# Weight conversion spread over VectorE, ScalarE and GpSimd, and two elementwise steps moved to GpSimd, in an mLSTM cell with a multiplicative feed-forward block

## The chip, the cores and the metric

The kernel runs on one core of a Trainium2 chip. The core has five engines that run their own instruction streams in order: TensorE (PE, with its weight loads shown as PEld), VectorE (DVE), ScalarE (ACT), GpSimd (POOL) and SyncE (SP), which issues all DMA transfers of this kernel. The metric is device time of one execution in microseconds; lower is better. A profile is one execution recorded by the hardware profiler; its time is given beside its span.

## The reference

Two blocks follow each other. The first is an mLSTM cell over 4 batches, 8 heads, 768 steps and head dimension 40:

```python
for t in range(S):
    m_new = np.maximum(f_gate[:, :, t] + m, i_gate[:, :, t])
    f_stab = np.exp(f_gate[:, :, t] + m - m_new)
    i_stab = np.exp(i_gate[:, :, t] - m_new)
    C = f_stab * C + i_stab * np.einsum('bhd,bhe->bhde', vt, kt)
    n = f_stab * n + i_stab * kt
    h_tilde = np.einsum('bhde,bhe->bhd', C, qt)
    denom = np.maximum(np.abs(np.einsum('bhd,bhd->bh', n, qt)), 1.0)
    y[:, :, t] = sigmoid(o_gate[:, :, t]) * h_tilde / denom
```

Its output, as 3072 tokens of 320 features, goes through `((x @ w1) * (x @ w2)) @ w3 @ w_out` with a hidden width of 1024. The activations come as float32. The four weight matrices come as float64 and are turned into float32 on the chip.

## The kernel before, in words

**Units.** The sequence is cut into 6 chunks of 128 steps (two halves of 64) for each of 4 batches: 24 units, unit n being chunk n // 4 of batch n % 4. For a unit, `load` fetches k, q and v, and `load_u` fetches into `pw` a broadcast row of stabilised gate sums. `weights` turns `pw` into decay weights: eight Exps on ScalarE (L221) and two masks on GpSimd (L223). `turn` transposes k and q on TensorE. `scores` multiplies them into PSUM (`ss`) and multiplies by `pw` on VectorE (L243). `cell` scales v by gate weights on GpSimd (`vw`, L257), forms the chunk's contribution to the state (`pc`), decays the state on GpSimd (L268) and adds on VectorE (L271), applies q to the state (`pi`) and the scores to v (`ph`), and adds the two in `h` (L284, L291). Then it forms the denominator's reciprocal (L295 to L298), multiplies the sigmoid of the output gate by it (L300), and multiplies `h` by that product into `y` (L302). GpSimd copies the tail of `y` (L304), and `x_trans` transposes `y` into `xT`.

**Gates.** `gates_of` runs scans over the forget and input gates on VectorE, first for the first 128 steps, then for the other 640. It ends in three differences and sums (L367, L368, L372), whose transposes on TensorE give `aT` and `wT`, the biases and weights that the units use.

**Weights.** `fetch` loads a piece of float64 weights as pairs of 32-bit words into one of three `raw` buffers. `convert` calls `to_f32`, which takes the exponent (`ex`) and the mantissa (`ma`, with the low word added) apart by bit operations and multiplies them into the float32 destination: seven passes on VectorE (L146 to L152). There are 34 such pieces: ten of w1 and w2, 512 columns wide, eight of w_out, 320 wide, and sixteen of w3, 512 wide. A w3 piece is transposed (`w3_trans`) and multiplied with w_out (`w3_mm`), so that the block's last two products become one with `w3o`.

**Feed-forward.** `ffn_up` computes one 128-wide slice of the hidden layer for a group of four units (`pa`, `pb`; copy on ScalarE, L428; product on VectorE, L429). `ffn_out` multiplies by `w3o` and stores.

**Order.** A loop over 30 steps writes units, conversions (list `n_cvt`), `ffn_up` and `ffn_out` (lists `n_up`, `n_down`) side by side; a planner in the tile framework then orders each engine's stream by its own estimate of durations and adds the semaphores. Streams are in order, so an instruction waits for all that stands ahead of it on its engine. Three things tie the steps together: `ss`, `pc` and `pi` share one PSUM buffer; qT, kT, vw and y have two buffers each; and a load waits in SyncE's queue until its buffer is free, with all later loads behind it.

Of the kernel before, what the change touches and what calls it, by code (L numbers as in the profile page):

```python
# [8 lines left out]
FP = mybir.dt.float32  # L9
U32 = mybir.dt.uint32  # L10
AF = mybir.ActivationFunctionType
OP = mybir.AluOpType
# [3 lines left out]
def kernel(  # L16
# [25 lines left out]
    nc = tc.nc  # L42

    B, H, S, D = q.shape
    L = 64
    P = 128
# [7 lines left out]
    BH = B * H  # L54
# [8 lines left out]
    const = ctx.enter_context(tc.tile_pool(name="const", bufs=1))  # L63
# [62 lines left out]
    wr = const.tile([2 * REM, DFF], FP, name="wr")  # L126
    w3o = const.tile([128, FO, DM], FP, name="w3o")
    CW = 512
    w1_d, w2_d, w3_d, wo_d = (x.bitcast(U32) for x in (moe_w1, moe_w2, moe_w3, moe_w_out))

    def raw_tile(n, pieces):
# [5 lines left out]
    def to_f32(dst, raw):  # L137


        n = dst.shape[-1]  # L140
        lo, hi = raw[:, :, 0], raw[:, :, 1]
        ex = wst.tile([128, n], U32, name="ex", tag="ex", bufs=1)
        ma = wst.tile([128, n], U32, name="ma", tag="ma", bufs=1)
        mf = ma.bitcast(FP)
        V = nc.vector
        V.tensor_scalar(out=ex, in0=hi, scalar1=20, scalar2=0x7FF, op0=OP.logical_shift_right, op1=OP.bitwise_and)  # L146
        V.tensor_scalar(out=ex, in0=ex, scalar1=896.0, scalar2=0.0, op0=OP.subtract, op1=OP.max)
        V.tensor_scalar(out=ex, in0=ex, scalar1=254.0, scalar2=float(1 << 23), op0=OP.min, op1=OP.mult)
        V.scalar_tensor_tensor(out=ex, in0=hi, scalar=0x80000000, in1=ex, op0=OP.bitwise_and, op1=OP.bitwise_or)  # L149
        V.tensor_scalar(out=ma, in0=hi, scalar1=0xFFFFF, scalar2=0x100000, op0=OP.bitwise_and, op1=OP.bitwise_or)  # L150
        V.scalar_tensor_tensor(out=mf, in0=lo, scalar=2.0 ** -32, in1=ma, op0=OP.mult, op1=OP.add)  # L151
        V.scalar_tensor_tensor(out=dst, in0=mf, scalar=2.0 ** -20, in1=ex.bitcast(FP), op0=OP.mult, op1=OP.mult)  # L152

    def cols(c0, n):
        return slice(2 * c0, 2 * (c0 + n))
# [89 lines left out]
    def cell(n):  # L245
        c, b = divmod(n, B)
        pw, vt, kt = u_t.pop(n), vbuf[n % NB], kbuf[n % NB]
        qT = qT_t.pop(n)
        first, second, after = state[b]
        state[b] = after, second, first  # L250
        hs = slice(b * H, (b + 1) * H)
        quarters = ((0, 0), (1, 1), (0, 1), (1, 0))


        ends = range(2 if c < NT2 - 1 else 1)
        vw = sb.tile([P, H, D1], FP, name="vw", tag="vw")
        nc.gpsimd.tensor_tensor(out=vw, in0=vt, in1=wT[:, c, hs].unsqueeze(2).to_broadcast([P, H, D1]), op=OP.mult)  # L257
        _, pc = two_banks("pc", D1)
        for p in range(NP):
            for x, e in quarters:  # L260
                if x in ends:
                    nc.tensor.matmul(pc[halves[e], x, p, :], lhsT=kt[halves[x], 2 * p + e, :],  # L262
                                     rhs=vw[halves[x], 2 * p + e, :], start=True, stop=True)

        def next_state(new, old, x):
            c1 = 2 * c + x - (2 if c else 0)
            if (c, x) > (0, 0):
                nc.gpsimd.tensor_tensor(out=new, in0=old, op=OP.mult,  # L268
                                        in1=dec_of[min(c, 1)][:, b * NP:(b + 1) * NP, c1:c1 + 1]
                                        .to_broadcast([P, NP, D1]))  # L270
                nc.vector.tensor_tensor(out=new, in0=pc[:, x], in1=new, op=OP.add)  # L271
            else:
                nc.vector.tensor_copy(out=new, in_=pc[:, x])

        next_state(second, first, 0)
        if len(ends) > 1:
            next_state(after, second, 1)
        h = sb.tile([P, H, D1], FP, name="h", tag="h")
        _, pi = two_banks("pi", D1)
        for p in range(NP):  # L280
            for hip, x in quarters:
                r, t = halves[hip], halves[x]
                nc.tensor.matmul(pi[t, hip, p, :], lhsT=qT[r, p, t], rhs=(first, second)[x][r, p, :], start=True, stop=True)  # L283
        nc.vector.tensor_tensor(out=h.rearrange("p (n two) d -> p two n d", two=2), in0=pi,  # L284
                                in1=gT[:, c, hs].rearrange("p (n two) -> p two n", two=2).unsqueeze(3)
                                .to_broadcast([P, 2, NP, D1]), op=OP.mult)
        ph = tps([P, H, D1], "ph")
        for hd in range(H):
            for r in halves:
                nc.tensor.matmul(ph[r, hd, :], lhsT=pw[r, hd, :], rhs=vt[r, hd, :], start=True, stop=True)  # L290
        nc.vector.tensor_tensor(out=h, in0=ph, in1=h, op=OP.add)  # L291


        den = sb.tile([P, H, 1], FP, name="den", tag="den")
        nc.vector.tensor_scalar(out=den.bitcast(U32), in0=h[:, :, D:D1].bitcast(U32), scalar1=0x7FFFFFFF, scalar2=None,  # L295
                                op0=OP.bitwise_and)
        nc.vector.tensor_scalar(out=den, in0=den, scalar1=1.0, scalar2=None, op0=OP.max)
        nc.vector.reciprocal(out=den, in_=den)  # L298
        e = o_t[n // GT][:, n % GT]
        nc.vector.tensor_tensor(out=e, in0=e, in1=den.to_broadcast([P, H, D]), op=OP.mult)  # L300
        y_t[n] = sb.tile([P, DM + REM], FP, name="y", tag="y")
        nc.vector.tensor_tensor(out=y_t[n][:, 0:DM].rearrange("p (h d) -> p h d", d=D), in0=h[:, :, 0:D], in1=e,  # L302
                                op=OP.mult)
        nc.gpsimd.tensor_copy(out=y_t[n][:, DM:DM + REM], in_=y_t[n][:, KF * P:DM])  # L304
# [12 lines left out]
    with tc.tile_pool(name="gates", bufs=1) as gates:  # L317
        f_sb = gates.tile([BH, S], FP, name="f_sb")
        a = gates.tile([BH, S], FP, name="a")
# [30 lines left out]
        def gates_of(c0, c1, then=None):  # L350
            n = c1 - c0
            rs = slice(c0 * L, c1 * L)
            f3, F3, U3, a3, w3d = (x.rearrange("p (c t) -> p c t", t=L)[:, c0:c1] for x in (f_sb, F, U, a, w))
            nc.vector.tensor_tensor_scan(out=F[:, rs], data0=on[:, rs], data1=f_sb[:, rs], initial=0.0,
                                         op0=OP.mult, op1=OP.add)

            nc.vector.memset(f3[:, :, 0:1], -1.0e30)
            nc.vector.tensor_tensor_scan(out=U[:, rs], data0=f_sb[:, rs], data1=a[:, rs], initial=0.0,
                                         op0=OP.add, op1=OP.max)
            nc.vector.tensor_tensor_scan(out=M[:, c0 + 1:c1 + 1], data0=F3[:, :, L - 1], data1=U3[:, :, L - 1],  # L360
                                         initial=M[:, c0:c0 + 1], op0=OP.add, op1=OP.max)
            before = M[:, c0:c1].unsqueeze(2).to_broadcast([BH, n, L])
            nc.vector.tensor_tensor(out=U3, in0=U3, in1=before, op=OP.subtract)
            nc.vector.tensor_tensor(out=U[:, rs], in0=U[:, rs], in1=F[:, rs], op=OP.max)
            last = nc.vector.tensor_tensor(out=U[:, rs], in0=F[:, rs], in1=U[:, rs], op=OP.subtract)
            nc.sync.dma_start(out=(U_rest if c0 else U_first).rearrange("c r t -> r c t"), in_=U3)
            nc.vector.tensor_tensor(out=a3, in0=a3, in1=before, op=OP.subtract)  # L367
            nc.vector.tensor_tensor(out=a[:, rs], in0=a[:, rs], in1=F[:, rs], op=OP.subtract)  # L368
            gate_cols(a, aT, c0 // 2, c1 // 2)
            if then:  # L370
                then()
            nc.vector.tensor_tensor(out=w3d, in0=a3, in1=U3[:, :, L - 1:L].to_broadcast([BH, n, L]), op=OP.add)  # L372

            nc.scalar.activation(out=dec[:, c0:c1], in_=U3[:, :, L - 1], func=AF.Exp)
            dec_d = dram.tile([2, B * NP, n], FP, name=f"dec_d{n}")
            nc.sync.dma_start(out=dec_d.rearrange("two n c -> n two c"), in_=dec[:, c0:c1])
            for x in range(2):
                nc.sync.dma_start(out=dec_of[min(c0, 1)][halves[x]].rearrange("p n c -> p (n c)"),
                                  in_=dec_d.rearrange("two n c -> two (n c)")[x:x + 1].to_broadcast([L, B * NP * n]))
            nc.scalar.activation(out=g[:, rs], in_=U[:, rs], func=AF.Exp)  # L380
            nc.scalar.activation(out=w[:, rs], in_=w[:, rs], func=AF.Exp)
            gate_cols(w, wT, c0 // 2, c1 // 2)
            gate_cols(g, gT, c0 // 2, c1 // 2)
            return last
# [127 lines left out]
```

## Time and profile before

| | |
|---|---|
| median of three runs | 547.93 us (547.26 to 551.87) |
| profiled execution | 551.33 us, span 549.7 us |
| TensorE busy | 504.5 us (92%) |
| VectorE busy | 252.2 us (46%) |
| ScalarE busy | 154.8 us (28%) |
| GpSimd busy | 86.5 us (16%) |
| mean granted TensorE clock | 0.969 |

The page gives busy times of engines, then the span in 40 equal slices with a digit for tenths of busy time, then groups of instructions. A group's line has the source line, engine, operation, the tiles written and read, the count, and behind the bar the busy time in us, the mean in ns and the idle time before it. A line of waits has who waited, for whom, the total in us, how many times, and the longest. A stage line has for each engine the busy us and the number of instructions, then the granted clock, the DMA engines' busy share and GB/s.

### The profile page before, as it was taken

To read this page: it belongs to the slowest core of one execution; us is meant where nothing else is said; L and a number is where in the kernel's file an instruction comes from. 1 tells how busy PE (TensorE), PEld (TensorE's weight loads), DVE (VectorE), ACT (ScalarE), POOL (GpSimd) and SP (SyncE) were. 2 spreads that over 40 slices of the span, in tenths; PEclk is the share of its full clock that TensorE was granted. 3 is DMA by queue.
4 is the path that set the end of the run, shared out by engine and by line. 5 is a ranking of instruction groups with operands and counts; after the bars stand their busy time and mean duration, and the time that the engine had idled before them with its cause. 6 is when DMAs were issued, how large, how long until landed. Compare 5 with 4: busy or idle time off the path is not lost.

```text
span 549.7 us, 11023 instructions
## 1 busy us (share of the span) xinstructions
PE 504.5 (92%) x4538; PEld 304.9 (55%) x4538; DVE 252.2 (46%) x568; ACT 154.8 (28%) x385; POOL 86.5 (16%) x157
## 2 busy tenths in 40 slices
PE   3547988988999999999989999999999999999997
PEld 3445666566545645545545765555555355353675
DVE  7849899789658557657532303322231200101000
ACT  2435544442630343333152313212111111111100
POOL 2523333233121111111211302110000000000000
PEclk9967989699999999999999999999999999999999
DMA  7799978678254174142142312200000000000011
GB/s 168 135 166 197 193 164 170 144 180 176 72 131 118 51 147 121 52 93 50 29 84 45 69 48 58 54 13 13 13 2 25 0 24 15 10 19 7 21 38 37
DMA packets 113042, 43.32 MB, mean 79 GB/s; under 512 B 102304, under 2 KB 105504, under 8 KB 112992
## 3 DMA queue, kind: packets, MB, share of 16 engines
q1 hardware_dynamic: 112992, 42.61, 35.1%
q8 instruction: 36, 0.59, 0.5%
q14 instruction: 14, 0.11, 0.1%
HBM read 38.57 MB, written 4.03 MB: 77 GB/s over the span
## 4 chain that ended last, share of the span: by engine, by line
PE 74%; DVE 13%; issue 4%; POOL 3%; ACT 2%; DMA 2%; SPq 1%; POOLq 0%; DVEq 0%; ACTq 0%
PE po L434 19%; PE pa L423 13%; PE pb L423 13%; PE pa L426 8%; PE wp L208 6%; PE ph L290 3%; PE pi L283 3%; PE pc L262 3%; PE pt L230 2%; DVE pw L243 2%; PE ss L241 2%; DVE ma L151 2%; PE px L313 1%; DMA pw<-U_rest 1%; DVE ex L149 1%
## 5 line engine op out<-in xcount | busy, mean ns | idle before, releaser
L429 DVE TENSOR_TENSOR ab<-pb,a_sb 128x512 f32<-128x512 f32 (+1 forms) x56 | 34.3, 612 | 201.9 <-ACT a_sb L428 119.5
L434 PE MATMUL po<-w3o,ab 128*128 128x320 f32 x384 | 105.8, 433 | 0.0
L423 PE MATMUL pa<-xT,w 128*128 128x512 f32 (+1 forms) x224 | 100.8, 564 | 1.4 <-ACT xT L314 1.4
L423 PE MATMUL pb<-xT,w 128*128 128x512 f32 (+1 forms) x224 | 95.6, 547 | 0.0
L434 PEld LDWEIGHTS po<-w3o,ab 128*128 128x128 f32 x384 | 72.0, 190 | 30.1 <-issue 1.5
L221 ACT ACTIVATE pw<-pw,aT 128x64 f32<-128x64 f32 x192 | 51.9, 341 | 65.5 <-DMA pw<-U_rest 51.2
L428 ACT COPY a_sb<-pa 128x512 f32<-128x512 f32 (+1 forms) x56 | 29.2, 521 | 144.6 <-PE pb L426 137.0
L423 PEld LDWEIGHTS pb<-xT,w 128*128 128x128 f32 x224 | 42.4, 195 | 35.6 <-issue 32.3
L426 PE MATMUL pa<-xT,wr 64*128 64x512 f32 (+1 forms) x112 | 57.1, 590 | 0.0
L426 PE MATMUL pb<-xT,wr 64*128 64x512 f32 (+1 forms) x112 | 57.1, 590 | 0.0
L423 PEld LDWEIGHTS pa<-xT,w 128*128 128x128 f32 x224 | 38.3, 194 | 29.9 <-issue 24.6
L257 POOL TENSOR_TENSOR vw<-vbuf,wT 128x328 f32<-128x328 f32 x24 | 22.3, 933 | 150.2 <-PE pc L262 83.3
L223 POOL TENSOR_SCALAR_AFFINE_SELECT pw<-pw 64x512 f32<-64x512 f32 x48 | 33.2, 692 | 57.8 <-ACT pw L221 52.6
L208 PE MATMUL wp<-wo,w3T 128*128 128x320 f32 x128 | 38.0, 452 | 0.3
L426 PEld LDWEIGHTS pa<-xT,wr 64*128 64x128 f32 x112 | 16.9, 189 | 35.5 <-issue 35.3
L437 ACT COPY o_sb<-po 128x320 f32<-128x320 f32 x24 | 10.2, 426 | 87.3 <-PE po L434 84.7
L208 PEld LDWEIGHTS wp<-wo,w3T 128*128 128x128 f32 x128 | 24.5, 197 | 10.6 <-DVE w3T L202 1.1
L290 PE MATMUL ph<-vbuf,pw 64*64 64x41 f32 x768 | 29.8, 233 | 0.0
L268 POOL TENSOR_TENSOR state<-state,dec 128x164 f32<-128x164 f32 x40 | 21.7, 544 | 41.0 <-PE pi L283 31.1
L283 PEld LDWEIGHTS pi<-state,qT 64*64 64x64 f32 x768 | 14.8, 144 | 24.1 <-issue 21.6
L290 PEld LDWEIGHTS ph<-vbuf,pw 64*64 64x64 f32 x768 | 27.1, 142 | 1.9 <-issue 0.8
L283 PE MATMUL pi<-state,qT 64*64 64x41 f32 x768 | 17.5, 239 | 10.8 <-DVE state L271 10.7
(79 smaller groups left out, 514.7 us busy)
## 6 DMA issues: line engine op xcount, KB each, us to landing
raw<-in_moe_w_dram SPq DMA_DIRECT2D x24, 512.0 KB, 4.7
pw<-U_rest SPq DMA_DIRECT2D x40, 128.0 KB, 3.7
kbuf<-in_k_dram SPq DMA_DIRECT2D x24, 160.0 KB, 4.1
qbuf<-in_q_dram SPq DMA_DIRECT2D x24, 160.0 KB, 3.8
vbuf<-in_v_dram SPq DMA_DIRECT2D x24, 160.0 KB, 4.0
o_in<-in_o_gate_dram SPq DMA_DIRECT2D x24, 160.0 KB, 3.5
out_dram<-o_sb SPq DMA_DIRECT2D x24, 160.0 KB, 1.8
raw<-in_moe_w_out_dram SPq DMA_DIRECT2D x8, 320.0 KB, 3.6
```

Of the source, the lines that this page charges most:

```text
L208: nc.tensor.matmul(wp, lhsT=w3T[:, ki, :], rhs=wo[:, ki, :], start=(ki == 0), stop=(ki == FO - 1))
L221: nc.scalar.activation(out=pw[:, h, :], in_=pw[:, h, :], func=AF.Exp, bias=aT[:, c, b * H + h:b * H + h + 1])
L223: nc.gpsimd.affine_select(out=pw[r], in_=pw[r], compare_op=OP.is_ge, fill=0.0, base=0, pattern=[[0, H], [1, L]], channel_multiplier=-1)
L257: nc.gpsimd.tensor_tensor(out=vw, in0=vt, in1=wT[:, c, hs].unsqueeze(2).to_broadcast([P, H, D1]), op=OP.mult)
L268: nc.gpsimd.tensor_tensor(out=new, in0=old, op=OP.mult, in1=dec_of[min(c, 1)][:, b * NP:(b + 1) * NP, c1:c1 + 1] .to_broadcast([P, NP, D1]))
L283: nc.tensor.matmul(pi[t, hip, p, :], lhsT=qT[r, p, t], rhs=(first, second)[x][r, p, :], start=True, stop=True)
L290: nc.tensor.matmul(ph[r, hd, :], lhsT=pw[r, hd, :], rhs=vt[r, hd, :], start=True, stop=True)
L423: nc.tensor.matmul(p, lhsT=wt[:, cc, fs], rhs=pick(x[:, cc, :]), start=(cc == 0), stop=False)
L426: nc.tensor.matmul(p, lhsT=wr[r, fs], rhs=pick(x[r, KF, :]), start=False, stop=True)
L428: nc.scalar.copy(out=a_sb, in_=pa)
L429: nc.vector.tensor_tensor(out=pick(ab), in0=pb, in1=a_sb, op=OP.mult)
L434: nc.tensor.matmul(po, lhsT=ab_t[gr][:, f, j * P:(j + 1) * P], rhs=w3o[:, f, :], start=(f == 0), stop=(f == FO - 1))
```

## The change

In `to_f32`, ScalarE computes the clamp of the exponent from below, as Relu with a bias of −896 from a small constant tile `low`, and converts the mantissa to float32 scaled by 2 to the −20. VectorE keeps five passes. GpSimd makes the last product of mantissa and exponent. The exponent's scratch tile is gone: the destination itself holds it. The mantissa's scratch tile has two buffers in place of one. In `cell`, the product of output gate and reciprocal runs on GpSimd. In `gates_of`, two differences and a sum run on GpSimd for the later 640 steps and stay on VectorE for the first 128.

```diff
+    low = const.tile([128, 1], FP, name="low")
+    nc.vector.memset(low, -896.0)
...
-        ex = wst.tile([128, n], U32, name="ex", tag="ex", bufs=1)
-        ma = wst.tile([128, n], U32, name="ma", tag="ma", bufs=1)
+        ex = dst.bitcast(U32)
+        ma = wst.tile([128, n], U32, name="ma", tag="ma")
         mf = ma.bitcast(FP)
         V = nc.vector
         V.tensor_scalar(out=ex, in0=hi, scalar1=20, scalar2=0x7FF, op0=OP.logical_shift_right, op1=OP.bitwise_and)
-        V.tensor_scalar(out=ex, in0=ex, scalar1=896.0, scalar2=0.0, op0=OP.subtract, op1=OP.max)
-        V.tensor_scalar(out=ex, in0=ex, scalar1=254.0, scalar2=float(1 << 23), op0=OP.min, op1=OP.mult)
+        nc.scalar.activation(out=dst, in_=ex, func=AF.Relu, bias=low)
+        V.tensor_scalar(out=ma, in0=hi, scalar1=0xFFFFF, scalar2=0x100000, op0=OP.bitwise_and, op1=OP.bitwise_or)
+        nc.scalar.activation(out=mf, in_=ma, func=AF.Copy, scale=2.0 ** -20)
+        V.scalar_tensor_tensor(out=mf, in0=lo, scalar=2.0 ** -52, in1=mf, op0=OP.mult, op1=OP.add)
+        V.tensor_scalar(out=ex, in0=dst, scalar1=254.0, scalar2=float(1 << 23), op0=OP.min, op1=OP.mult)
         V.scalar_tensor_tensor(out=ex, in0=hi, scalar=0x80000000, in1=ex, op0=OP.bitwise_and, op1=OP.bitwise_or)
-        V.tensor_scalar(out=ma, in0=hi, scalar1=0xFFFFF, scalar2=0x100000, op0=OP.bitwise_and, op1=OP.bitwise_or)
-        V.scalar_tensor_tensor(out=mf, in0=lo, scalar=2.0 ** -32, in1=ma, op0=OP.mult, op1=OP.add)
-        V.scalar_tensor_tensor(out=dst, in0=mf, scalar=2.0 ** -20, in1=ex.bitcast(FP), op0=OP.mult, op1=OP.mult)
+        nc.gpsimd.tensor_tensor(out=dst, in0=mf, in1=dst, op=OP.mult)
...
-        nc.vector.tensor_tensor(out=e, in0=e, in1=den.to_broadcast([P, H, D]), op=OP.mult)
+        nc.gpsimd.tensor_tensor(out=e, in0=e, in1=den.to_broadcast([P, H, D]), op=OP.mult)
...
-            nc.vector.tensor_tensor(out=a3, in0=a3, in1=before, op=OP.subtract)
-            nc.vector.tensor_tensor(out=a[:, rs], in0=a[:, rs], in1=F[:, rs], op=OP.subtract)
+            eng = nc.gpsimd if c0 else nc.vector
+            eng.tensor_tensor(out=a3, in0=a3, in1=before, op=OP.subtract)
+            eng.tensor_tensor(out=a[:, rs], in0=a[:, rs], in1=F[:, rs], op=OP.subtract)
...
-            nc.vector.tensor_tensor(out=w3d, in0=a3, in1=U3[:, :, L - 1:L].to_broadcast([BH, n, L]), op=OP.add)
+            eng.tensor_tensor(out=w3d, in0=a3, in1=U3[:, :, L - 1:L].to_broadcast([BH, n, L]), op=OP.add)
```

## The prediction

> **What bounds the kernel now.** I read the page first: the engines' totals and its 40 slices of 13.74 us.
>
> ```profile
> PE 504.5 (92%) x4538; PEld 304.9 (55%) x4538; DVE 252.2 (46%) x568; ACT 154.8 (28%) x385; POOL 86.5 (16%) x157
> ...
> PE   3547988988999999999989999999999999999997
> ...
> DVE  7849899789658557657532303322231200101000
> ...
> PEclk9967989699999999999999999999999999999999
> DMA  7799978678254174142142312200000000000011
> ```
>
> TensorE is full from the twelfth slice on; before that VectorE and the DMA engines are the full ones. The stage view puts numbers on it (busy us and counts for PE, PEld, DVE, ACT, POOL; then clock, DMA share, GB/s):
>
> ```profile
> 0.00:21.00 21.00, 6.62 (x56) 5.02 (x56) 15.90 (x39) 9.62 (x27) 8.52 (x26) 1.00 0.88 179
> 21.00:60.00 39.00, 26.81 (x505) 22.24 (x506) 29.18 (x68) 14.32 (x36) 12.22 (x19) 0.78 0.86 162
> 60.00:110.00 50.00, 43.94 (x586) 30.90 (x584) 44.40 (x110) 24.12 (x60) 15.70 (x25) 0.86 0.80 166
> 110.00:160.00 50.00, 45.80 (x551) 30.59 (x550) 41.25 (x95) 20.60 (x56) 13.18 (x20) 1.00 0.62 150
> 160.00:550.00 390.00, 381.31 (x2845) 216.16 (x2843) 121.51 (x259) 86.11 (x207) 36.90 (x68) 1.00 0.19 45
> ```
>
> After 160 us TensorE idles 390 − 381.3 = 8.7 us, over 3 of them in the drain, so nothing taken off VectorE there can pay. Before 160 us it idles 14.4 + 12.2 + 6.1 + 4.2 = 36.9 us, and a lowered clock stretches 26.8 us of its work by 0.22 and 43.9 us by 0.14, about 12 us. That is all there is to win. TensorE's waits in 21 to 160 us (line waited for, us, times, longest) say for whom:
>
> ```profile
> PE pi L283 <- DVE state L271: 10.7, 9, 2.4
> PE px L313 <- DVE y L302: 5.4, 3, 4.5
> PE pc L262 <- DVE pw L243: 4.6, 6, 1.4
> ```
>
> 20.7 of the 22.5 us of idleness there end on VectorE, which is 75 to 89% busy. But the chain also runs over SyncE's queue: issues of 2 to 3 us each show its transfers backed up nearly without a break from 26 to 66 and 72 to 106 us. Those stretches shorten only where a buffer is freed sooner.
>
> **What the Trainium skill says.** (1) "SBUF — State Buffer", section "Who interferes with whom": VectorE and GpSimd share a port pair; a VectorE operation with two SBUF inputs, or a tensor_scalar in a 2-port mode, and a GpSimd operation that reads SBUF exclude each other. The trace agrees (ns min/median/max):
>
> ```profile
> L148 DVE TENSOR_SCALAR ex<-ex x34: 311/418/953, 7.7 to 268.8; 128x512 uint32<-128x512 uint32 x26, 128x320 uint32<-128x320 uint32 x8
> L257 POOL TENSOR_TENSOR vw<-vbuf,wT x24: 734/847/2754, 15.3 to 385.8; 128x328 f32<-128x328 f32 x24
> ```
>
> One conversion pass more than doubles, one vw takes 2.75 us instead of 0.73. Operations with one input in PSUM (L243, L271, L284, L291, L429) are free of this by the page; the trace has L271 at 313 to 329 ns over all 40, however busy GpSimd is. (2) "ScalarE: Activation LUTs", section "Table sets": relu and copy lie in every table set, so no table load is added; the built stream has the same 13 loads. (3) "TensorE: Matmul & The Clock Gate", section "What's actually happening": about 3.4 us of idleness halves the clock. The records agree in kind, 0.57 at 40 to 50 us after the waits there and 0.50 at 100 to 110 us after some 3 us of gaps near 97.
>
> **The change, part by part.** The profiled execution took 551.33 us (span 549.7), the median of the three runs is 547.93; I sum against 551.3 and carry the difference to the median.
>
> ```profile
> L152 DVE SCALAR_TENSOR_TENSOR w<-ma,ex 128x512 f32<-128x512 f32 x24 | 17.3, 720 | 0.9
> L147 DVE TENSOR_SCALAR ex<-ex 128x512 uint32<-128x512 uint32 x26 | 11.3, 435 | 0.0
> L300 DVE TENSOR_TENSOR o_in<-o_in,den 128x320 f32<-128x320 f32 x24 | 12.1, 504 | 0.6
> ```
>
> Conversion: VectorE goes from seven passes to five. L147 (435 ns) and L152 (720 ns) leave: 1.155 us for each of 26 tiles of 512, 0.408 + 0.483 = 0.89 us for each of 8 of 320, 37 us in all. 22 of the 34 tiles (14 and 8) come before 160 us: 16.2 + 7.1 = 23.3 us. L300 leaves 24 × 0.504 = 12.1 us, ten of them early, 5.0 us. L367, L368 and L372 for the later chunks (0.81 + 0.81 + 0.87) leave 2.5 us. Together 31 of the 131 us that VectorE is busy before 160 us.
>
> ScalarE gets two passes a tile. The ScalarE page, section "What ACT_TABLE_LOAD costs", prices an ACTIVATE at 186 ns + 0.833 ns an element, 93 more with a bias pointer, 93 overlapped: an estimate of 1.13 us for both passes at 512 and 0.81 at 320. The trace's 341 ns for a 64-element Exp with bias fits. 14 × 1.13 + 8 × 0.81 = 22 us on top of 68.7 us before 160 us: 57% busy. No bound; the cost is order, since VectorE's third pass waits for Relu, which queues behind Exps that wait for pw transfers.
>
> GpSimd: vw at 328 elements takes 0.73 us undisturbed, the state decay at 164 takes 0.46, so 0.19 us + 1.65 ns an element: 1.03 us at 512. "GPSIMD Engine Reference", section 3.1, has 4497 ns at 2048, or 1.12. I take 1.1, and 0.72 at 320. Before 160 us: 14 × 1.1 + 8 × 0.72 + 10 × 0.72 for the output gate + 3 × 1.35 for the 640-element gate steps = 32.4 us on top of 49.6: 51% busy. So VectorE loses 31 us and GpSimd gains 32 us of work on a shared port; the gain can only come from what runs beside PSUM-fed work and from VectorE's queue being shorter in front of the steps that TensorE waits for.
>
> Stage by stage, path gains positive:
> - To 21 us: the three gate steps go ahead of the first two vw in GpSimd's queue, and the later chunk's f_sb transposes ahead of the second ss on TensorE. Three steps of 1.35 us, disturbed by scans and 640-element steps on VectorE, make the first pw 0.5 to 2.5 us later. But in the old queue the second pw (26.5 us) stood behind four conversion passes although its input was there at 22.5; those are mostly gone. Net 0 (−2 to +1).
> - 39 to 60 us: y of unit 0 stands behind five or six conversion passes (h done 40.3, y at 43.2); in the new queue behind two. 2.5 us on paper, but the Exps of unit 3 need a pw whose issue ends at 42.2 and lands about 3.5 us later. +1.
> - 60 to 160 us: pi and pc wait 9.6 us for VectorE. Five conversion passes of seven remain, and fewer stand right ahead of L271. A third to a half goes: +4.
> - SyncE stands 5.6 us at 66.7 to 72.3 waiting for y of unit 3 to free an o_in buffer. Earlier y: +2 (0 to 3).
> - GpSimd's queue: L155 of the changed kernel (mf times dst) stands ahead of affine and decay in units 0 to 3: −1 (0 to −4).
> - Port collisions of 32 new us on GpSimd: −1.5 (0 to −8).
> - Clock: a half-speed window costs about 5 us and may go or come: +1 (−5 to +5).
> - After 160 us: 0. y comes some 0.3 us later (0.72 for 0.49, and a hand-over), but px reads the unit before (in the trace, px at 178.16, its y at 157.9). Conversions have a whole 19.7 us step. If that cover failed, 0.3 × 15 units = 4.5 us.
>
> Sum +5.5: 545.8 us against 551.3; the same 1.0% off the median gives 542.4. VectorE's chains gain a little more than single terms show, because an earlier y and raw release feed the next unit: I say 541.5.
>
> **Rivals.** *Nothing measurable* (546 us): the backed-up transfers pace 26 to 106 us anyway. For: DMA share 0.80 to 0.86 there, and the Exps wait 17 us for pw. Against: the SyncE pauses come from VectorE. Gain only after 106 us: about 2 us. *GpSimd becomes the chain* (558 us, slower): its stream runs in order, so the product (1.1 us) and output gate (0.72, itself waiting for the reciprocal) hold the mask, vw and decay behind them, and VectorE's y waits for GpSimd in turn. If this hits each of the first ten units with no cover, 10 × 1.8 = 18 us against the 5.5 plus port losses already counted: about +10. It decides when collisions push vw from its mean of 0.93 us past about 1.3, with GpSimd over 70% busy before 160 us. *Both clock dips go and the chain shortens* (530 us): 5.5 + 12. "It doesn't do what it says" is excluded: the built streams show the moved operations.
>
> **How the numbers follow.** Forecast case 0.45 (535 to 545), nothing measurable 0.26 (543 to 553), GpSimd bound 0.21 (554 to 567), large gain 0.08 (525 to 535). One per cent, 5.5 us, is about what a measurement of this kernel tells from no change. Of the forecast case three quarters lie below 542.4: faster 0.34 + 0.08 = 0.42, same 0.11 + 0.26 = 0.37, slower 0.21. The range, 531 to 557, leaves out half of the large gain and some 0.12 of the slow case.
>
> **What would show it.** Right: VectorE near 200 us in total; GpSimd near 140; TensorE waits on L271's successor below 7 us before 160 us; the step at which TensorE becomes full (px at 158.5 us) some 6 us earlier, and the rest of the span unchanged. Wrong: vw or affine with a mean well above 0.93 and 0.69 us, TensorE waiting for pc or pi whose chain ends on GpSimd, a new half-clock window, or idleness of TensorE after 160 us above 9 us.

## The result and the profile after

The changed kernel took **572.7 us** (median of four runs, 571.56 to 574.09) against 547.8 for the kernel before: a ratio of 1.0449, with a 95% interval of 1.0395 to 1.0502. The forecast was 541.5 us with a range that ended at 557. The change costs 25 us where a gain of 6 was expected. The profiled execution took 571.56 us (span 569.9).

The changed kernel's page, engines' totals and slices (of 14.25 us here):

```profile
PE 510.4 (90%) x4538; PEld 309.1 (54%) x4538; DVE 224.5 (39%) x474; ACT 193.9 (34%) x453; POOL 147.3 (26%) x218
...
PE   4366987888999997999998999999999999999997
...
DVE  7727669688375464365451312223320300000000
...
PEclk9999999898999998999999999999999999999999
DMA  8799489866342353441323413110000000000010
```

VectorE fell by 28 us and not by 52, GpSimd rose by 61. TensorE's granted clock is better than before (0.988 against 0.969), so a lowered clock is not the answer. The stage view of the changed kernel, at the boundaries used before:

```profile
0.00:21.00 21.00, 6.84 (x56) 5.08 (x56) 15.71 (x35) 8.76 (x20) 11.86 (x27) 1.00 0.95 184
21.00:60.00 39.00, 24.81 (x396) 21.11 (x397) 21.91 (x45) 21.40 (x54) 19.29 (x25) 1.00 0.94 173
60.00:110.00 50.00, 42.65 (x646) 30.81 (x645) 37.16 (x84) 31.74 (x76) 28.79 (x40) 0.97 0.75 139
110.00:160.00 50.00, 44.06 (x494) 29.71 (x495) 33.37 (x75) 28.53 (x67) 19.05 (x29) 0.93 0.53 123
160.00:550.00 390.00, 375.44 (x2888) 211.02 (x2887) 116.36 (x237) 101.78 (x234) 68.30 (x101) 1.00 0.21 48
```

VectorE is less busy in each stage, and TensorE has not become busier for it. After 160 us TensorE idles 390 − 375.4 = 14.6 us, against 8.7 before. Fixed clock boundaries mix different work, so I also followed one landmark, the copy that ends the transpose of a unit's y (L314 before, L317 after). Unit 8's copy starts at 160.12 us before and at 171.25 after. From there to unit 15's copy the stage in which the w3 pieces are converted takes 141.28 and 150.41 us. After unit 15 nothing more is lost. So about **11 us go before unit 8 and 9 us in the w3 stage**; the rest of the 25 is the difference between profiled executions and medians (the profiled one is among the slow ones of its kernel before, and the fastest after).

TensorE's waits from 21 to 160 us in the changed kernel, the same three as shown before:

```profile
PE pi L286 <- DVE state L274: 11.1, 8, 2.2
PE pc L265 <- DVE pw L246: 4.2, 7, 1.6
...
PE px L316 <- DVE y L305: 2.3, 1, 2.3
```

The wait for pi, 10.7 us before, was forecast to shrink and did not. In the w3 stage, where the forecast had no loss, TensorE's waits are, before (160.1 to 301.4 us)

```profile
PE pc L262 <- DVE pw L243: 3.7, 7, 1.7
PE pa L423 <- ACT xT L314: 0.9, 1, 0.9
```

and after (171.2 to 321.7 us)

```profile
PE pc L265 <- DVE pw L246: 7.3, 7, 3.1
PE pi L286 <- DVE state L274: 4.3, 5, 1.0
PE pa L427 <- ACT xT L317: 1.4, 1, 1.4
```

So two steps of VectorE come later there than TensorE needs them: the state add that pi waits for, and the score product (L246), which reads ss and so frees the PSUM buffer that pc takes. What VectorE and SyncE wait for up to unit 8 (21 to 160.1 us before) adds to this. The kernel before:

```profile
DVE state L271 <- POOL state L268: 5.3, 7, 2.5
...
SPq L112 <- DVE y L302: 5.6, 1, 5.6
```

The changed kernel (21 to 171.2 us):

```profile
DVE state L274 <- POOL state L271: 11.0, 7, 4.8
...
DVE y L305 <- POOL o_in L303: 4.6, 6, 0.8
...
DVE w L153 <- ACT w L149: 2.6, 3, 1.4
...
SPq L112 <- DVE y L305: 12.1, 1, 12.1
```

The state add waits twice as long for GpSimd's decay. SyncE stands 12.1 us, not 5.6, before it may load the next output gates into a buffer that y releases, with the raw weights behind it; but most of the difference is that SyncE comes to that point sooner (at 61.8 us against 66.7), and the load goes out only 1.7 us later (73.97 against 72.32).

### The profile page after: what moved, and what is told of

Read it like the earlier page. It is cut to its first block, busy times and chain, and to the rows that moved or that the text cites. A ratio compares the mean times of both kernels' runs of the same rounds, so it can differ in the third digit from the quotient of the medians.

```text
span 569.9 us, 11065 instructions
## 1 busy us (share of the span) xinstructions
PE 510.4 (90%) x4538; PEld 309.1 (54%) x4538; DVE 224.5 (39%) x474; ACT 193.9 (34%) x453; POOL 147.3 (26%) x218
## 4 chain that ended last, share of the span: by engine, by line
PE 59%; DVE 13%; POOL 6%; issue 4%; ACT 4%; DMA 4%; SPq 1%; POOLq 0%; DVEq 0%; ACTq 0%
PE po L438 18%; PE pa L427 12%; PE pb L427 11%; PE pa L430 7%; DVE w L154 3%; DMA raw<-in_moe_w_dram 2%; PE pi L286 2%; PE wp L211 2%; PE pt L233 2%; DVE ma L152 2%; POOL w L155 1%; POOL vw L260 1%; PE pc L265 1%; PE ph L293 1%; DVE pw L246 1%
## 5 line engine op out<-in xcount | busy, mean ns | idle before, releaser
L427 PE MATMUL pa<-xT,w 128*128 128x512 f32 (+1 forms) x224 | 102.6, 570 | 1.4 <-ACT xT L317 1.4
L155 POOL TENSOR_TENSOR w<-ma,w 128x512 f32<-128x512 f32 x24 | 33.1, 1380 | 63.3 <-DVE w L154 48.4
L260 POOL TENSOR_TENSOR vw<-vbuf,wT 128x328 f32<-128x328 f32 x24 | 20.7, 864 | 72.8 <-issue 37.7
L303 POOL TENSOR_TENSOR o_in<-o_in,den 128x320 f32<-128x320 f32 x24 | 17.7, 737 | 64.9 <-DVE den L301 64.8
L151 ACT ACTIVATE ma<-ma 128x512 f32<-128x512 uint32 (+1 forms) x34 | 19.9, 589 | 38.6 <-DVE ma L150 38.5
L286 PE MATMUL pi<-state,qT 64*64 64x41 f32 x768 | 17.8, 241 | 16.5 <-DVE state L274 16.4
L152 DVE SCALAR_TENSOR_TENSOR ma<-raw,ma 128x512 f32<-128x512 uint32 (+1 forms) x34 | 28.6, 841 | 9.5 <-ACT ma L151 9.4
```

Source lines behind the costliest of these rows:

```text
L152: V.scalar_tensor_tensor(out=mf, in0=lo, scalar=2.0 ** -52, in1=mf, op0=OP.mult, op1=OP.add)
L155: nc.gpsimd.tensor_tensor(out=dst, in0=mf, in1=dst, op=OP.mult)
L427: nc.tensor.matmul(p, lhsT=wt[:, cc, fs], rhs=pick(x[:, cc, :]), start=(cc == 0), stop=False)
```

## The experiments

Three theories stood at the start. The **queue theory**: GpSimd runs in order, so the product L155 holds up vw and the decay behind it. The **hand-over theory**: VectorE stands idle until ScalarE's passes are done. The **gate theory**: y and the first units wait for steps moved to GpSimd. A fourth, the **port theory**, came when these did not suffice: the product does its harm by holding up VectorE's access to SBUF while it runs. All ratios are against the kernel before on the same chip; "unit 8" and "w3 stage" are the two times in us defined above, from the one profiled execution of each kernel (before: 160.1 and 141.3 us). The w3 stage repeats to about 1 us (140.2 to 141.3 in the kernels whose conversion and output gate stay on VectorE); unit 8 is less certain, since executions of the kernel before range over 8 us.

| kernel | ratio, 95% interval | median us | unit 8 | w3 stage |
|---|---|---|---|---|
| the change | 1.0449, 1.0395 to 1.0502 | 572.7 | 171.3 | 150.4 |
| conversion alone | 1.0436, 1.0383 to 1.0488 | 572.2 | 172.2 | 148.8 |
| ScalarE's share alone | 1.0219, 1.0179 to 1.0258 | 559.8 | 164.1 | 146.2 |
| change, product on VectorE | 1.0315, 1.0259 to 1.0370 | 565.3 | 171.4 | 146.4 |
| both gate parts alone | 1.0115, 1.0054 to 1.0177 | 555.0 | 164.6 | 142.8 |
| scratch in destination | 1.0057, 1.0036 to 1.0078 | 551.4 | 158.5 | 140.6 |
| change, w3 products on VectorE | 1.0397, 1.0325 to 1.0469 | 570.7 | 169.2 | 146.3 |
| change, decay on VectorE | 1.0414, 1.0365 to 1.0463 | 571.9 | 171.1 | 148.7 |
| before, decay on VectorE | 0.9956, 0.9929 to 0.9983 | 545.6 | 152.5 | 141.2 |
| idle product on GpSimd | 1.0640, 1.0583 to 1.0698 | 582.1 | 171.6 | 157.6 |
| one fill on GpSimd | 1.0175, 1.0117 to 1.0232 | 556.9 | 163.5 | 142.7 |
| three fills on GpSimd | 1.0235, 1.0156 to 1.0313 | 562.4 | 167.0 | 144.0 |
| gate differences alone | 1.0065, 1.0036 to 1.0094 | 551.6 | 163.8 | 140.2 |
| output gate alone | 1.0082, 1.0053 to 1.0110 | 553.1 | 159.6 | 142.0 |
| clamp on ScalarE | 1.0112, 1.0071 to 1.0154 | 554.3 | 158.4 | 145.6 |
| mantissa on ScalarE | 1.0025, 1.0001 to 1.0049 | 551.2 | 160.0 | 141.2 |
| scratch and decay | 0.9955, 0.9924 to 0.9986 | 546.3 | 154.3 | 140.4 |

### Which part of the change

**Conversion alone.** The changed kernel with the gate parts back:

```diff
-        nc.gpsimd.tensor_tensor(out=e, in0=e, in1=den.to_broadcast([P, H, D]), op=OP.mult)
+        nc.vector.tensor_tensor(out=e, in0=e, in1=den.to_broadcast([P, H, D]), op=OP.mult)
...
-            eng = nc.gpsimd if c0 else nc.vector
+            eng = nc.vector
```

> The changed kernel with the output gate and the later gates' differences back on VectorE: only the weight conversion is shared out. Three theories of the 25 us. Queue theory: GpSimd runs in order, and the 1.3 us products stand ahead of vw and of the state decay, which pc and pi of TensorE wait for; in the stage of the w3 pieces (after 160 us) this costs about 1.1 us a step. Then this kernel keeps nearly all of the loss, 565 to 572 us, and a step after 160 us stays at 20.5 to 20.8 us instead of 19.7. Hand-over theory: the two passes on ScalarE hold VectorE and the raw buffers; it expects the same total, so this run does not part it from the first. Gate theory: y waits for GpSimd's output gate, which releases the o_in and raw transfers late; then this kernel gets most of the loss back, 548 to 555 us.

It has the whole loss, 1.0436. The gate theory falls as the main cause, and so does SyncE's longer pause: here it is 6.9 us, and that load goes out at 70.1 us, earlier than in the kernel before.

**Both gate parts alone.** The kernel before with those two edits the other way.

> The kernel before with only the output gate and the later gates' differences on GpSimd; the conversion stays on VectorE. Queue theory and hand-over theory: no products, so TensorE's steps after 160 us stay at 19.7 us and the total is within 4 us of the kernel before (545 to 552 us). Gate theory: the first pw and the early y come late as in the changed kernel, 8 to 12 us before 160 us, so 556 to 562 us or more.

1.0115, some 6 us: between the two expectations. By themselves the gate parts cost; added to the shared conversion they cost nothing measurable (1.0449 against 1.0436).

**The product on VectorE.** The changed kernel with

```diff
-        nc.gpsimd.tensor_tensor(out=dst, in0=mf, in1=dst, op=OP.mult)
+        V.tensor_tensor(out=dst, in0=mf, in1=dst, op=OP.mult)
```

> The changed kernel with the conversion's last product on VectorE instead of GpSimd (0.7 us for 128x512 by the like pass of the kernel before); ScalarE's two passes, the output gate and the gate differences stay moved. Queue theory: GpSimd's queue holds vw and the decay no longer back, steps after 160 us return to 19.7 us (about 10 us back) and part of the early loss too: 548 to 556 us. Hand-over theory: VectorE still stands for ScalarE twice a tile and gets a pass back, so the loss stays or grows, 570 us or more. Gate theory: the loss before 160 us stays (11 us), 558 to 563 us.

1.0315: no theory had it. The w3 stage gives back 4 us. Up to unit 6 the run is 2.9 us late where the changed kernel is 9.6 late, so the product costs 6.7 us there. Then TensorE is busy for 1.8 of the 4 us from 132 to 136 and runs at clock 0.50 from 136 to 148, and unit 7 ends 10.7 us late; the gain is gone. This is one execution, the slowest of the four, so the stretch need not be in the others.

**ScalarE's share alone.** Both edits above together: the product, the output gate and the gate differences are on VectorE, ScalarE keeps its two passes.

> Only ScalarE's share of the conversion: Relu and the scaled copy on ScalarE, the last product, the output gate and all gate differences on VectorE. VectorE has six passes a tile instead of seven. Queue theory: nothing is added to GpSimd, so no loss after 160 us; before it VectorE is some 9 us less busy: 543 to 549 us. Hand-over theory: the loss before 160 us comes from VectorE standing for ScalarE in each tile, so 556 us or more. Gate theory: 545 to 549 us.

1.0219, 12 us: the hand-over theory's number, and the queue theory alone can't be right. Putting the product on GpSimd on top of this (conversion alone) costs 0.0217 × 547.5 = 12 us more. The two halves of the conversion's loss are about equal (each with an uncertainty of 2 to 4 us).

Where did the moved product's time go? The groups of VectorE's sign pass and mantissa pass, with ScalarE's share alone:

```profile
L152 DVE SCALAR_TENSOR_TENSOR ma<-raw,ma 128x512 f32<-128x512 uint32 x26 | 18.8, 725 | 2.2 <-ACT ma L151 1.6
L154 DVE SCALAR_TENSOR_TENSOR w<-raw,w 128x512 uint32<-128x512 uint32 x24 | 17.4, 723 | 0.3
L155 DVE TENSOR_TENSOR w<-ma,w 128x512 f32<-128x512 f32 x24 | 17.1, 712 | 0.1
```

and with the product on GpSimd (conversion alone):

```profile
L154 DVE SCALAR_TENSOR_TENSOR w<-raw,w 128x512 uint32<-128x512 uint32 x24 | 24.4, 1015 | 0.6
L152 DVE SCALAR_TENSOR_TENSOR ma<-raw,ma 128x512 f32<-128x512 uint32 x26 | 21.9, 842 | 8.9 <-ACT ma L151 8.7
```

L155 leaves VectorE, 17.1 us here and 23.6 with the narrower pieces. But L154 grows by 7.0 us and L152 by 3.1, others too, and VectorE's total goes only from 240.9 to 237.8 us. **Of 23.6 us moved away, 20.5 came back** as longer passes, and L152's wait for ScalarE grew by 7.1 us besides.

### Queue or port

**w3 products on VectorE.** The changed kernel with the product of the w3 pieces alone on VectorE:

```diff
-    def to_f32(dst, raw):
+    def to_f32(dst, raw, prod=None):
...
-        nc.gpsimd.tensor_tensor(out=dst, in0=mf, in1=dst, op=OP.mult)
+        (prod or nc.gpsimd).tensor_tensor(out=dst, in0=mf, in1=dst, op=OP.mult)
...
-            to_f32(dst, raw)
+            to_f32(dst, raw, nc.vector)
```

> The changed kernel with the product of the sixteen w3 pieces alone on VectorE; the other eighteen stay on GpSimd. Queue theory: in the stage of the w3 pieces the decay no longer stands behind two products, TensorE's wait for pi falls from 4.3 to below 2 us there, and the stage (unit 8 to unit 15) takes 146 us instead of 150.4; before it nothing changes. 566 to 569 us. If GpSimd's products cost nothing there (the order of the streams does): 571 to 574 us.

The w3 stage came out at 146.3 us and its wait for pi at 1.6 us, as expected; the median, 570.7 us with runs from 565.7 to 573.9, decides nothing.

**The decay on VectorE**, in the changed kernel and in the kernel before:

```diff
-            nc.gpsimd.tensor_tensor(out=new, in0=old, op=OP.mult,
+            nc.vector.tensor_tensor(out=new, in0=old, op=OP.mult,
```

> The changed kernel with the decay of the state on VectorE, so that GpSimd is no longer on the way from pc to pi, while it keeps all its products. Queue theory: TensorE's waits for pi (16.4 us) fall by half or more; VectorE has 0.33 us more for each of some 40 decays: 562 to 568 us. Port or hand-over theory: pi waits for VectorE's own queue as long as before, 570 to 576 us.

> The kernel before with the decay of the state on VectorE, as a control of the run above. GpSimd has little to do there, so its queue holds nothing up; the hand-over to GpSimd and back goes, VectorE gets some 0.3 us for each decay: 545 to 550 us by every theory. Below 545 us would mean that the hand-over cost TensorE time already in the kernel before.

The queue theory failed here: with GpSimd off the way from pc to pi, 571.9 us remain, and pi still waits 14.9 us in all (16.4 in the changed kernel). In the kernel before the same edit gains 0.4%.

The trace shows how. One step of the w3 stage of the changed kernel, in order of time (start and length in us; the bracket is idle time and its releaser):

```profile
180.84 1.29 POOL L155 TENSOR_TENSOR w<-ma,w 128x512 f32<-128x512 f32 x1 [5.75 <-DVE w L154]
181.04 1.64 DVE L154 SCALAR_TENSOR_TENSOR w<-raw,w 128x512 uint32<-128x512 uint32 x1
...
182.82 1.32 POOL L155 TENSOR_TENSOR w<-ma,w 128x512 f32<-128x512 f32 x1 [0.69 <-DVE w L154]
...
183.71 0.98 DVE L152 SCALAR_TENSOR_TENSOR ma<-raw,ma 128x512 f32<-128x512 uint32 x1 [0.69 <-ACT ma L151]
184.10 1.18 POOL L260 TENSOR_TENSOR vw<-vbuf,wT 128x328 f32<-128x328 f32 x1
184.12 1.13 PE L427 MATMUL pa<-xT,w 128*128 128x512 f32 x2
184.61 0.32 DVE L274 TENSOR_TENSOR state<-pc,state 128x164 f32<-128x164 f32 x1
185.25 0.46 POOL L271 TENSOR_TENSOR state<-state,dec 128x164 f32<-128x164 f32 x1
185.74 0.33 DVE L274 TENSOR_TENSOR state<-pc,state 128x164 f32<-128x164 f32 x1 [0.81 <-POOL state L271]
...
186.21 0.68 PE L286 MATMUL pi<-state,qT 64*64 64x41 f32 x32 [0.96 <-DVE state L274]
```

L154 starts 0.2 us after GpSimd's product and takes 1.64 us instead of 0.69: it ends at 182.68, roughly its own length after the product has ended (182.13). That pushes L150 and L152 back; L152 waits 0.69 us for ScalarE's L151 and then meets vw. The first state add stands behind L152, the decay behind vw, the second add behind the decay, and pi behind that. The kernel before, same step:

```profile
172.17 0.32 DVE L271 TENSOR_TENSOR state<-pc,state 128x164 f32<-128x164 f32 x1
...
172.66 1.98 PE L423 MATMUL pa<-xT,w 128*128 128x512 f32 x4
...
173.92 0.32 DVE L271 TENSOR_TENSOR state<-pc,state 128x164 f32<-128x164 f32 x1
...
174.57 0.68 PE L283 MATMUL pi<-state,qT 64*64 64x41 f32 x32
```

Four pa matmuls (1.98 us) cover the second state add; in the changed kernel the planner put pi behind two of them (1.13 us). So the state came later and its cover had been cut. Either alone would have cost little here: behind four matmuls pi would have waited about 0.1 us (an estimate, 186.21 − 184.12 − 1.98) instead of 0.96, and with the product of the w3 pieces on VectorE, still behind two, it waits 1.6 us in the whole stage instead of 4.3. In the run with the decay on VectorE the step has the same stretched L154 and L152, and pi waits 0.74 us for VectorE's own queue.

The stretching can be read pass by pass. In the changed kernel seven L154 passes of 512 columns ran beside a product and nothing else of GpSimd's: 1.64 us each. The twelve that ran beside no GpSimd work took 0.69.

To tell queue and port apart for the whole kernel I left the product on VectorE (ScalarE's share alone) and gave GpSimd work behind each piece that nobody's result depends on.

```diff
+        nc.gpsimd.tensor_tensor(out=mf, in0=mf, in1=dst, op=OP.mult)
```

> ScalarE's share alone (559.8 us measured), the product on VectorE, and a second product of the same size on GpSimd behind it whose result nobody reads: it overwrites the mantissa's scratch. It adds work to the kernel; TensorE waits for none of it. If the way of the data through GpSimd's queue was what cost 12 us (the product as something TensorE and the next unit wait for), vw and the decay still stand behind it, so 563 to 570 us, and the run with a fill in its place shows nearly the same. If the shared port was it, VectorE's passes stretch as they did (the pass that ORs in the sign 0.72 to about 1.0 us) and the time is 566 to 575 us, well above the run with the fill.

```diff
+        nc.gpsimd.memset(mf, 0.0)
```

> As the run above, but GpSimd fills the mantissa's scratch with zeros instead of making the second product: an instruction at the same place of GpSimd's queue, behind the same wait, that reads nothing from SBUF. It adds work to the kernel. Port theory: VectorE's passes keep their lengths (the pass that ORs in the sign near 0.72 us) and the time stays at 558 to 563 us. Queue theory: about the same as the run above, shorter only by as much as the fill is shorter than the product.

The fill three times over:

> As the run with one fill on GpSimd behind each piece (556.9 us, a fill of 128x512 took 0.56 us), but three fills: some 1.7 us in GpSimd's queue, more than a product's 1.3 undisturbed, and still nothing read from SBUF. Adds work to the kernel. Port theory: VectorE's passes keep their lengths and the time stays within 4 us of the one fill, 555 to 562 us. Queue theory: vw and the decay stand behind as much as with the product, so most of its 25 us come, 570 us or more.

The Trainium skill, "SBUF — State Buffer", section "Who interferes with whom", says that a VectorE instruction with two SBUF inputs contends with a GpSimd instruction that reads SBUF, "not with one that only writes it". The runs agree: nine L154 passes that ran beside fills alone took 0.68 to 0.69 us. The idle product:

```profile
L156 POOL TENSOR_TENSOR ma<-ma,w 128x512 f32<-128x512 f32 x24 | 36.1, 1503 | 76.3 <-DVE w L155 76.3
L152 DVE SCALAR_TENSOR_TENSOR ma<-raw,ma 128x512 f32<-128x512 uint32 x26 | 24.5, 943 | 0.7
```

The three fills:

```profile
L152 DVE SCALAR_TENSOR_TENSOR ma<-raw,ma 128x512 f32<-128x512 uint32 x26 | 18.4, 707 | 7.7 <-ACT ma L151 7.7
...
L156 POOL MEMSET ma<- 128x512 f32 x26 | 14.5, 559 | 65.0 <-DVE w L155 64.2 <-DVE wr L155 0.7
...
L157 POOL MEMSET ma<- 128x512 f32 x26 | 14.3, 548 | 1.0
L158 POOL MEMSET ma<- 128x512 f32 x26 | 13.6, 523 | 0.9
```

Three fills hold GpSimd's queue for 0.559 + 0.548 + 0.523 = 1.63 us a piece, longer than the product's 1.50, and end at 1.0235. The product ends at 1.0640: 0.0405 × 547.5 = **22 us (give or take 5) come from what the product does besides standing in the queue**, which is to read SBUF. In both runs pi stands behind the same number of pa matmuls in the w3 stage, so this is not the planner's order of them. What the place in the queue costs cannot be told from nothing: three fills are some 3 us above one fill and 1 us above none (1.0219), with overlapping intervals.

The 22 us are not all VectorE's longer passes: its busy time is 256.1 us against 245.5. In the w3 stage pi waits 11.7 us against 3.3, and four stretches of 3.4 us at half clock follow such waits of 1.9 to 2.6 us, so that TensorE is busy 142.0 us there against 135.2. VectorE also waits 6.9 us for the mantissa's scratch to come free (3.1 us with three fills), which explains part, not most, of the 22. The changed kernel has one half-clock stretch in that stage, as the kernel before has, so the 22 us are not a measure of its own loss.

Three things were off in the expectations: the stretched pass is L152 here, not the sign pass, because the work beside the product differs; the product's 582 us exceeded its upper number; and one fill (556.9 us) came out below, three fills (562.4) just above theirs.

### ScalarE's share

Three runs take the 12 us of that share apart; they do not settle it. **Scratch alone**: the kernel before, with

```diff
-        ex = wst.tile([128, n], U32, name="ex", tag="ex", bufs=1)
-        ma = wst.tile([128, n], U32, name="ma", tag="ma", bufs=1)
+        ex = dst.bitcast(U32)
+        ma = wst.tile([128, n], U32, name="ma", tag="ma")
```

> The kernel before with one thing of the change: the exponent's scratch is the destination itself and the mantissa's scratch has two buffers; all seven passes stay on VectorE, in their old order, and no other engine gets anything. The share on ScalarE alone had cost 12 us (559.8 against 547.7), some 4 us before 160 us, 5 in the stage of the w3 pieces and some in the gates' part. Hand-over theory: that came from VectorE standing for ScalarE's passes, which are not here, so 546 to 550 us and a stage of w3 pieces (x transpose of unit 8 to that of unit 15) of 141 us as before. Order theory: the first pass now needs a free destination and the planner writes another order of all streams; then a good part of the 12 us is here too, 553 to 560 us, with 143 to 146 us for that stage.

1.0057, 3 us, between the two expectations, and the w3 stage as before. **The clamp on ScalarE**, on top of that, with the constant tile `low`:

```diff
-        V.tensor_scalar(out=ex, in0=ex, scalar1=896.0, scalar2=0.0, op0=OP.subtract, op1=OP.max)
+        nc.scalar.activation(out=dst, in_=ex, func=AF.Relu, bias=low)
```

> The kernel before with the scratch in the destination (551.4 us by itself) and only the clamp from below on ScalarE; the mantissa's path stays on VectorE, all else as before. VectorE's next pass waits for ScalarE once a piece instead of twice. If each hand-over costs alike, about half of the 12 us: 552 to 556 us. If the clamp's hand-over is what counts (VectorE waited 5.7 us for it and 2.2 us for the mantissa's): 556 to 561 us. If the mantissa's does: 548 to 552 us.

**The mantissa's copy on ScalarE**: ScalarE's share alone with the clamp back on VectorE.

> Of ScalarE's share only the mantissa's scaled copy on ScalarE; the clamp and the last product are on VectorE, which keeps seven passes a piece, as the kernel before; the new order of passes stays. The clamp alone gave 554.3 us and both 559.8. If the two hand-overs add: 556 to 559 us (the kernel with the scratch alone 551.4, plus some 5 to 6). If the mantissa's wait is hidden by VectorE's other passes: 550 to 553 us.

Clamp 1.0112, mantissa 1.0025, both 1.0219: they do not add up. The clamp costs 4 to 5 us in the w3 stage, the mantissa none. The planner may have a hand in it, though no run changes its order alone: with the clamp on ScalarE pi stands behind two pa matmuls and waits; with clamp, mantissa and one fill it stands behind four, and the w3 stage takes 142.7 us instead of 146.2, although GpSimd has more to do. How much of ScalarE's 12 us is the hand-over and how much the order that the planner makes of it stays open.

### The gate parts one by one, and a version that is faster

**The gate differences alone**, in the kernel before:

> The kernel before with only the later gates' differences and sum on GpSimd; the output gate stays on VectorE. Both together had cost 7 us (555.0 against 547.7), 2 to 3 of them by unit 0 to 3 and 1.5 in the stage of the w3 pieces. If the gate differences make the first units late and the output gate costs the rest: 549 to 552 us, unit 0 2 us late, and 141 us for the w3 stage. If the output gate is all of it: 546 to 549 us. If the differences are all of it: 553 to 557 us.

**The output gate alone**, in the kernel before:

> The kernel before with only the output gate's product on GpSimd. With the gate differences it was 555.0 us, the differences alone 551.6. If the two add: 550 to 553 us, with some 1.5 us in the stage of the w3 pieces, where y waits for GpSimd. If y's 0.3 us is hidden there, as the forecast had it: 546 to 549 us.

The differences cost 0.65%, with unit 0 3.0 us late; the output gate 0.82%, with 0.7 us in the w3 stage, no more than the scatter there. Their sum, 1.5%, lies within the interval of both together.

**Scratch and decay**: the kernel before with the scratch edit and the decay on VectorE.

> A version that may beat both kernels: the kernel before with the exponent's scratch in the destination, two buffers for the mantissa, and the decay of the state on VectorE; GpSimd and ScalarE get nothing. The decay alone gave 545.6 us against 547.5, the scratch alone 551.4 in the median though 547.3 in its profiled span. If the two are independent: 546 to 551 us. If the extra buffer lets VectorE's shorter way from pc to pi pay: 541 to 545 us.

0.9955, no better than the decay alone. The decay on VectorE, with nothing of the change, is the best version measured, 0.4% faster than the kernel before.

## Why the prediction was wrong

**Three steps failed: the price of the port, ScalarE's passes entered at nothing, and "After 160 us: 0".** The first two are the two halves of the loss, some 12 us each; the third is where 9 us of them fall. What the product does to VectorE's passes is shown; how much of what follows is the planner's order, and why ScalarE's passes cost so much, stays open. Each in turn, then the rest.

- *Port collisions −1.5 (0 to −8).* This term was mis-sized. The product's whole cost on top of ScalarE's share is 12 us, of which 6 fall by unit 6 (8.1 us late against 2.3). The lock had been seen, in one vw of 2.75 us and one pass of 0.95; what was not asked is who would run beside the product. Because the planner interleaves two pieces, it is often the next piece's sign or mantissa pass, each with two SBUF inputs: 17 of the 34 products ran beside one of the two. With the other passes that grew, VectorE got 3 of 24 us.
- *ScalarE: "No bound; the cost is order".* The order was named and then entered in the sum at nothing, without a reason; the share costs 12 us, 5 of them in the w3 stage (146.2 us against 141.3). The size of a pass was about right: 0.717 us with the bias and 0.627 without, 1.34 for both, against an estimate of 1.13 net of overlap from the Trainium skill's "ScalarE: Activation LUTs", section "What ACT_TABLE_LOAD costs". How the 12 us come about, by VectorE's waits or by the planner's order, the runs do not settle.
- *After 160 us: 0.* The w3 stage lost 9 us. "Conversions have a whole 19.7 us step" looked only at when a piece must be finished. It did not look at what stands behind a conversion pass in VectorE's queue: the state add that pi waits for (no wait before, 4.3 us after) and the score product ahead of pc (3.7 and 7.3 us). The cover named, px reading the unit before, concerns y alone; the product of the output gate alone costs at most 0.7 us there, so that sentence held. The fallback of 4.5 us was for y too.
- *60 to 160 us: pi and pc +4.* Not there: from 21 to 160 us pi waits 11.1 us where it waited 10.7. VectorE has fewer passes, but L154 and L152 are longer, and GpSimd's decay came into the chain (state add waiting for the decay: 5.3 to 11.0 us).
- *SyncE's pause of 5.6 us: +2.* The pause is 12.1 us. y now waits for GpSimd's product, and the load behind it goes out 1.7 us later, not earlier. The conversion alone shows that the loss does not need this.
- *To 21 us: net 0 (−2 to +1).* Unit 0 is 1.9 us late, and 3.0 with the differences alone. A gate step on GpSimd took 1.27 to 1.99 us, not 1.35.
- *39 to 60 us: +1.* Unit 1 is 5.2 us late; the differences and the product share this.
- *Affine and decay behind L155: −1.* Neither confirmed nor refuted; by the fills the queue costs at most some 3 us, not clear of noise.
- *Clock +1.* The better clock came (0.97 up to unit 8, 0.90 before), but no gain from it is seen: TensorE's records up to unit 8 are 5.3 us longer (128.6 against 123.3 us for the same number of instructions), which I can't explain, and its idle time is 5.8 us longer. The prediction's reading of "some 3 us of gaps near 97" was also off: TensorE has one gap of 1.36 us there, and the last before it, of 1.8 us, is at 88. So this trace does not show that it takes 3.4 us of idleness; with the idle product, too, half clock followed gaps of 1.9 to 2.6 us.
- *GpSimd's product 1.1 us.* Its median is 1.29 us (shortest 1.25) and its mean 1.38 at 512 columns, 0.87 at 320; the output gate took 0.74, about as estimated.

The rival "GpSimd becomes the chain" had the sign and, at 558, less than half of the loss. Its own signs did not come: vw's mean is 0.86 us, not above 1.3, and GpSimd is busy 79 of the first 160 us, 49% and not 70. VectorE's passes became longer, beside an engine that was half idle. Of the signs of being wrong that the prediction named, two came: TensorE idles more than 9 us after 160 us (14.6), and GpSimd's decay stands in the chain that pi waits for.

## What to carry to other kernels

Before moving an elementwise pass from VectorE to GpSimd, look at what VectorE would run beside it: where that often had two SBUF inputs, as here, VectorE kept only 3 of the 24 us saved, while its steps that read PSUM kept their lengths, and so did its two-input passes beside GpSimd work that only writes. And of a queue that is relieved ask not its total, but which instruction that the bottleneck waits for stands behind the passes that remain: here the state add, which in the step shown of the kernel before was done only 0.3 us before TensorE took up pi. A pass handed to another engine and back belongs in the sum with its wait, not only with its length.

## What the runs showed of the hardware that I had not expected

- GpSimd work as long as a product but without reads left VectorE's passes with two SBUF inputs at their lengths (L152 at 707 ns beside three fills, 943 beside the product). Some passes with one SBUF input were held up by fills all the same: an L150 took 0.82 us and an L153 0.83, where both take 0.42 alone.
- VectorE's operations with one input in PSUM kept their lengths in the changed kernel: the state add 323 ns before and 324 after, the score product 682 and 683.
- Beside a product, a pass with two SBUF inputs hardly advanced: one of 0.69 us took 1.64 when it began 0.2 us after a product of 1.29, and one took 1.80 beside 1.27 in the run with the idle product.
- Reducing VectorE's busy time by 28 us, with a better clock, made the kernel 25 us slower.
